# First batch of a banded attention with a feed-forward layer: attention weights and x turned on TensorE in float32, float32 weighted sums

## The chip, the cores and the metric

The kernel runs on one core of a Trainium2 chip. The metric is the device time of one execution in microseconds. Engines are named as the profile names them: PE (TensorE matmuls), PEld (its weight loads), DVE (VectorE), ACT (ScalarE), POOL (GpSimd), SP (the queue that issues the DMAs).

## The reference

Four batches of 768 tokens, 8 heads of 64 columns, then a feed-forward layer with 2048 hidden columns on all 3072 tokens. Cut to what matters:

```python
scores = scale * q @ k.T + bias            # bias: -slope[h] * distance
scores = where(is_global | is_local, scores, -1e9)   # 8 first keys, and the 96 before a row
a = exp(scores - max(scores))
a = a / (sum(a) + 1e-9)
x = a @ v                                  # (3072 tokens, 512 columns)
h = x @ w_in                               # 512 x 2048
g = h * tanh(log1p(exp(h)))
out = g @ w_out                            # 2048 x 512
```

The two weights of the feed-forward layer reach the kernel as 64-bit words and are turned into two float16 halves on the chip.

## The kernel before

**Tiles.** The tokens are worked in 12 chunks of 256 (`ci` 0 to 11), three to a batch. In a chunk there are two blocks of 128 rows and 8 heads, that is 8 attention tiles of 128 rows and two heads each: `t` runs from 0 to 95, and `t` 0 to 23 is the first batch. A row sees one or two windows of 128 keys (`nk`: the block's own 128, and a gathered window of the 96 before and 32 first ones; only the first block of a batch has one alone). The feed-forward layer has 8 units to a chunk, `m` = 8 ci + fp, 96 in all; it needs 32 pieces of weights, 0.5 MB each: an even piece belongs to w_in, an odd one to w_out.

**One order, written by hand.** A string, `PROGRAM`, holds some 2,100 tokens, a letter and a number each; every token issues one step, and each engine executes its instructions in the order in which the tokens stand. A dash behind a token puts a step on DVE that else stands on ACT (copies) or POOL (subtractions). The letters that are spoken of below:

- `q` loads q and k, `v` loads v, `w` a piece of the weights; all DMAs are issued by SP.
- `h`, `l`: v as two float16 halves (ACT L150, DVE L216). `x`: the gathered window of v, copied by DMA from those halves and from the window before.
- `s`: scores of two tiles on PE (L377); in the first batch (`ci < CF32`, 3) one float32 product of q and k, in the others three float16 products of halves.
- `t`: bias and row maximum (DVE L391). `y`: exponential and row sum (ACT L400), which leaves the attention weights `A` in float32.
- `g`, `p`: `A` as two float16 halves `hl` (a copy on ACT L150 or DVE L148; a subtraction on POOL or DVE, both L154).
- `X`: `hl` turned by one transposing DMA into `AT` (L420). `W`: the weighted sum on PE, three float16 products for each head and window (L436), into the PSUM tile `pav`.
- `R`: division by the row sum, which leaves x in float32 (DVE L443, L445, L447). `T`, `U`: its two float16 halves `xhl`. `V`: `xhl` turned by a transposing DMA into `xT` (L464).
- `A`, `S`, `B`, `C`: a piece of the weights joined from its words into float32 (L150, L319 or L317, L323, L327). `D`, `E`: its two halves (L150 or L148; L154).
- `i`: the first layer of a unit on PE, 24 products into a PSUM tile `ph` (L481). `j u n r G H`: the activation (ACT L488 to L500, DVE L504, L508). `z`, `Z`: its halves. `o`: the second layer, 12 products (L526), into `po0`, `po1`, or for `ci` 1 into the `pav` tiles.

**PSUM.** `sc` and `ph` have two tiles each in rotation, `pav0`, `pav1`, `po0`, `po1` one each.

**The start.** All weights must be made from words once, and the first batch's attention lies beside that. On PE the first-batch steps stand ahead of most of the feed-forward units: when the unit step `o8` begins, PE has issued all of `s` 0 to 22, `W` 0 to 23, and the units' steps `i0 o0 i8 i1 i9`. The same set, plus the new steps, stands ahead of `o8` in the changed order too.

Of the kernel before, what the change touches and what calls it, by code (L numbers as in the profile page):

```python
# [114 lines left out]
def windowed(st, tc, loc):  # L115
# [447 lines left out]
    def checks(i):  # L563
# [39 lines left out]
        p15' t16 E2 p14 t17 E5' X13 X15 X14 i0 W13 s18 W14 W10 W15 q5 y16 y17 g16' R2 p16 E3 w7 w9 X16 j0 u0 n0 r0 g17 T2 p17 t18 t19 B6 G0 H0 U2 x2 s20 y18
        z0 A6 S6 y19 A7 A9 g18 g19 R3 B7 t21 S7' T3' B9 C6 U3 p18' t20 p19' D4 y21 S9 D6 y20 Z0 E4 X17 V2 X18 V3 o0 s22 W17 W16 W18 i8 w8 g21' C9 p21 t23 C7
        t22 D9 g20 D7 y22 y23 E6 p20' N0 X19 X21 X20 w10 B8 E7' g23' p23 A8 S8 j8 g22 u8 n8 r8 G8 p22 E9 i1 W21 W20 W19 i9 X23 X22 w11 w12 R4 H8 j1 T4 C8 U4
        G1 D8' z8 u1 S10 n1 A10 j9 u9 r1 n9 r9 S11 A11 A12 S12 W23 W22 Z8 E8 R5 B10 C10 w14 w13 w24 w25 w16 w15 D10' H1 G9 z1' B11 H9 C11 o8 E10 i2 i10 j2
# [207 lines left out]
```

## Time and profile before

| | |
|---|---|
| median of 3 runs | 643.12 us (643.02 to 644.0) |
| the profiled execution, its own time | 643.97 us |
| its span in the trace | 642.2 us |
| PE, DVE, ACT, POOL busy | 596.2, 466.7, 455.7, 171.9 us |
| matmul records | 5042, of which L481 2304, L526 1152, L436 1056 |
| DMA, all queues | 80.38 MB in 152,680 packets, 121,376 of them under 512 B |

The profiled execution stands 0.85 us above the median. Of an engine's share of busy time little can be read alone here, since the first 160 us of the span and the rest have different limits; the table of stretches that the prediction shows is the view to begin with.

### The profile page before, as it was taken

The page shows a single profiled execution, that of the slowest core. Times are in us where ns is not written, and L with a number is a line of the kernel's source. Part 1 is how long each engine was busy: PE and PEld are TensorE (multiplying, and loading weights), DVE is VectorE, ACT ScalarE, POOL GpSimd, SP SyncE. Part 2 cuts the span into 40 slices and gives each one's busy share as a digit, 9 for nine tenths or more (in the row PEclk, how much of TensorE's full clock was granted, in tenths as well). Part 3 has the DMA queues.
Part 4 walks back from the last instruction along what each step waited for, and adds up shares of the span by engine and source line. Part 5 has one row for each costly group of instructions (what it writes and reads, how often), then busy time and mean ns, then how long its engine had stood idle before and what let it go on. Part 6 is the DMA issues. An engine that isn't in the chain of part 4 may idle for free.

```text
span 642.2 us, 13678 instructions
## 1 busy us (share of the span) xinstructions
PE 596.2 (93%) x5042; PEld 403.3 (63%) x5042; DVE 466.7 (73%) x1207; ACT 455.7 (71%) x1109; POOL 171.9 (27%) x144
## 2 busy tenths in 40 slices
PE   3746888999999999999999999999999999999996
PEld 2535565656666677576766766666767666667672
DVE  6798899999968678885567879368786685552443
ACT  4658897977977768687687785667768778554651
POOL 1233363423122321340332221121213244111020
PEclk9999899999999999999999999999999999999998
DMA  8999999247526569445458539244424456510001
GB/s 224 255 216 217 222 306 347 57 143 195 141 66 136 120 126 207 90 96 137 79 108 181 138 76 209 66 85 109 67 50 100 66 83 117 87 12 1 34 2 36
DMA packets 152680, 80.38 MB, mean 125 GB/s; under 512 B 121376, under 2 KB 141856, under 8 KB 152608
## 3 DMA queue, kind: packets, MB, share of 16 engines
q1 hardware_dynamic: 152608, 79.46, 54.6%
q8 instruction: 40, 0.66, 0.4%
q14 instruction: 32, 0.26, 0.1%
HBM read 38.54 MB, written 6.29 MB: 70 GB/s over the span
## 4 chain that ended last, share of the span: by engine, by line
PE 69%; DVE 12%; DMA 6%; ACT 5%; issue 4%; SPq 2%; POOL 1%; DVEq 0%; POOLq 0%; ACTq 0%
PE po L526 30%; PE ph L481 30%; PE sc L377 5%; DMA AT<-hl 4%; PE pav L436 4%; DMA kr<-kd 2%; DVE gf L508 2%; DVE ws L327 1%; DVE ws L323 1%; DVE A L391 1%; SPq L420 1%; ACT A L400 1%; ACT e L488 1%; ACT u L492 1%; PE pav L526 1%
## 5 line engine op out<-in xcount | busy, mean ns | idle before, releaser
L481 PE MATMUL ph<-xT,wts 128*128 128x256 f16 x2304 | 265.1, 273 | 2.1 <-POOL wts L154 1.3
L481 PEld LDWEIGHTS <-wts 128*128 128x128 f16 x2304 | 222.6, 98 | 39.5 <-POOL wts L154 2.6
L526 PE MATMUL po<-wts,gt 128*128 128x512 f16 x1056 | 241.7, 381 | 0.9 <-POOL gt L154 0.7
L526 PEld LDWEIGHTS <-gt 128*128 128x128 f16 x1152 | 109.6, 98 | 130.5 <-POOL gt L154 5.5
L154 POOL TENSOR_TENSOR gt<-gf,gt 128x512 f16<-128x512 f32 x58 | 72.2, 1246 | 212.4 <-DVE gt L148 95.5
L488 ACT ACTIVATE e<-ph 128x512 f32<-128x512 f32 x96 | 56.6, 590 | 89.6 <-PE ph L481 88.8
L508 DVE CUSTOM_DVE_ANT_0 gf<-gf,r 128x512 f32<-128x512 f32 x96 | 78.2, 816 | 50.2 <-ACT r L500 46.5
L154 POOL TENSOR_TENSOR hl<-A,hl 128x512 f16<-128x512 f32 (+1 forms) x51 | 59.2, 1163 | 191.0 <-DVE hl L148 98.3
L400 ACT ACTIVATE A<-A,nm 128x256 f32<-128x256 f32 (+1 forms) x192 | 91.5, 478 | 23.3 <-DVE nm L391 22.8
L504 DVE SCALAR_TENSOR_TENSOR gf<-e,ph 128x512 f32<-128x512 f32 x96 | 65.1, 681 | 32.4 <-ACT e L488 32.3
L391 DVE CUSTOM_DVE_ANT_0 A<-sc,mb 128x256 f32<-128x256 f32 (+1 forms) x192 | 68.4, 395 | 27.0 <-PE sc L377 24.8
L500 ACT ACTIVATE r<-r 128x512 f32<-128x512 f32 x96 | 60.0, 625 | 2.1
L492 ACT ACTIVATE u<-e 128x512 f32<-128x512 f32 x96 | 60.1, 626 | 1.9
L496 ACT ACTIVATE r<-u 128x512 f32<-128x512 f32 x96 | 59.8, 624 | 2.0
L436 PEld LDWEIGHTS <-AT 128*128 128x128 f16 x1056 | 40.3, 101 | 31.6 <-DMA AT<-hl 21.2
L436 PE MATMUL pav<-vc,AT 128*128 128x64 f16 x480 | 34.5, 198 | 13.1 <-DMA AT<-hl 12.5
L436 PE MATMUL pav<-vo,AT 128*128 128x64 f16 x576 | 40.2, 199 | 4.0 <-DMA AT<-hl 3.3
L150 ACT ACTIVATE gt<-gf 128x512 f16<-128x512 f32 x44 | 27.3, 622 | 19.6 <-DVE gmax L508 18.4
L377 PE MATMUL sc<-kr,qr 64*128 64x256 f32 (+1 forms) x96 | 24.5, 571 | 16.5 <-DVE nm L391 8.2
L154 DVE TENSOR_TENSOR hl<-A,hl 128x512 f16<-128x512 f32 (+1 forms) x45 | 34.3, 763 | 6.4 <-ACT hl L150 6.1
L154 POOL TENSOR_TENSOR wts<-ws,wts 128x512 f16<-128x512 f32 x20 | 26.5, 1332 | 46.4 <-DVE wts L148 23.4
L400 ACT ACTIVATION_READ_ACCUMULATOR A<-A,nm 128x1 f32 x192 | 36.0, 187 | 0.0
(96 smaller groups left out, 522.3 us busy)
## 6 DMA issues: line engine op xcount, KB each, us to landing
kr<-kd SPq DMA_DIRECT2D x32, 208.0 KB, 4.1
qr<-qT SPq DMA_DIRECT2D x24, 256.0 KB, 3.3
wts<-w_in SPq DMA_DIRECT2D x12, 512.0 KB, 5.9
vr<-v SPq DMA_DIRECT2D x12, 512.0 KB, 4.6
wts<-w_out SPq DMA_DIRECT2D x12, 512.0 KB, 7.6
out<-ob SPq DMA_DIRECT2D x11, 512.0 KB, 3.6
vc<-vo SPq DMA_DIRECT2D x20, 192.0 KB, 3.0
kr<-kd SPq DMA_DIRECT2D x16, 144.0 KB, 3.9
```

The lines of the kernel that those rows point to most:

```text
L154: (nc.vector if other else nc.gpsimd).tensor_tensor(out, in_, high, op=ALU.subtract)
L391: nc.vector.tensor_tensor_reduce(out=A[:, j, 0:w], in0=sc[j][:, 0:w], in1=m, scale=-1.0 / (UNIT if ci < CF32 else UNIT * SQ), scalar=3.0e3 ...
L400: nc.scalar.activation(A[:, j], A[:, j], AF.Exp, bias=nm[:, h:h + 1], scale=-1.0, accum_out=rs[:, h:h + 1])
L436: nc.tensor.matmul(pav[:, cols], AT[:, (x * 2 + j) * nk + kk, :], vs[kk][:, y, cols], start=(n == 0), stop=(n == last))
L481: nc.tensor.matmul(ph[:, j, :].rearrange("p (b t) -> p b t", b=2), wv4[:, 2 * fb, x, c * P:(c + 1) * P], xT[:, :, y * NCC + c, :], start=( ...
L488: nc.scalar.activation(mish[m]["e"], mish[m]["h"], AF.Exp, scale=-1.0 / (SV * SW), accum_out=esum[:, m:m + 1])
L492: nc.scalar.activation(u, mish[m]["e"], AF.Square, bias=0.5)
L496: nc.scalar.activation(mish[m]["r"], mish[m]["u"], AF.Ln, bias=0.25 / RS, scale=1.0 / RS)
L500: nc.scalar.activation(r, r, AF.Exp, scale=-1.0)
L504: nc.vector.scalar_tensor_tensor(gf, mish[m]["e"], 0.5, mish[m]["h"], op0=ALU.add, op1=ALU.mult)
L508: nc.vector.tensor_tensor_reduce(out=gf, in0=gf, in1=mish[m]["r"], scale=SG / (SV * SW * RS), scalar=0.0, op0=ALU.mult, op1=ALU.max, accum ...
L526: nc.tensor.matmul(pos[ci][t], gt[:, x, j, t * P:(t + 1) * P], wv4[:, 2 * fb + 1, y, :], start=(fb == 0 and n == 0), stop=(fb == NFB - 1 a ...
```

## The change

For the chunks of the first batch (`ci < CF32`) alone:

- `g`, `p` and `X` are gone. A new step `P` turns `A` in float32 on PE (`turn_p`): a product with an identity matrix for each head and window, 128 x 128, two for a tile with one window and four for the others, 88 in all. The result goes to PSUM: `po0` and `po1` in turn for `t` below 16, a `ph` tile for `t` 16 to 23. A new step `F` copies it from there to `AT` in SBUF, on ACT, or on DVE with a dash.
- `W` makes one float32 product for each head and window (88 in all) where three float16 ones stood (264).
- `h` and `l` are gone. `v` loads into the tile that `W` reads, and `x` loads the gathered window from HBM with two or three DMAs. The factor of 256 that `h` applied is now applied in `R`.
- `V` is gone. A new step `O` turns x in float32 on PE into a `ph` tile, four products for a block of rows, 24 in all; `T` and `U` make the halves from that tile and write `xT`.
- A new step `I` makes the identity matrix on DVE.

In the built program each of the turns is one weight load and one matmul, and each float32 product, of `s` as of `W`, is two loads and two matmuls. The later batches keep their steps. The order of the tokens is another one: far from the old one up to the second batch, then with a few neighbours swapped; on PE it is the same from `W40` on.

PE, the program's first instructions. Before (`sc` are scores; AT is the turned weights):

```order
L377 MATMUL sc<-kr,qr 128x128 x4
L377 MATMUL sc<-kr,qr 128x256 x4
L436 LDWEIGHTS AT
L436 MATMUL pav_214<-vo,AT 128x64
```

and of the change:

```order
L399 MATMUL sc<-kr,qr 128x128 x4
L452 MATMUL po_177<-idn,A 128x128 x2
L399 MATMUL sc<-kr,qr 128x256 x4
L452 MATMUL po_186<-idn,A 128x128 x2
L474 MATMUL pav_210<-vo,AT 128x64 x2
L452 MATMUL po_213<-idn,A 128x128 x4
L399 MATMUL sc<-kr,qr 128x128 x4
L452 MATMUL po_224<-idn,A 128x128 x4
L474 MATMUL pav_245<-vc,AT 128x64
```

What PE did alone, scores and sums, is now in three steps: a turn stands between a tile's scores and its sum, and the next tile's scores stand between its turn and its sum.

SP, from the first loads on. Before:

```order
L172 DMA qr<-qT 128x2x256
L175 DMA kr<-kd 64x2x288 x2
L292 DMA wts<-w_in 128x4x256
L206 DMA vr<-v 128x2x512
L294 DMA wts<-w_out 128x1024
L420 DMA_TRANSPOSE AT<-hl 128x4x128
L420 DMA_TRANSPOSE AT<-hl 128x8x128
L226 DMA vc<-vo 96x1024
L227 DMA vc<-vo 32x1024
```

(rows that repeat are left out) and of the change:

```order
L172 DMA qr<-qT 128x2x256
L175 DMA kr<-kd 64x2x288 x2
L314 DMA wts<-w_in 128x4x256
L209 DMA vo<-v 128x2x512
L229 DMA vc<-v 96x512
L230 DMA vc<-v 32x512
L316 DMA wts<-w_out 128x1024
L232 DMA vc<-v 96x2x512
L234 DMA vc<-v 32x512 x2
```

The transposing DMAs, each of which stood in SP's queue until its `hl` was made, are gone from the first batch; what stands there now reads HBM and waits for no engine but for a free buffer.

DVE, around the second pair of tiles. Before (`hl` are the halves of A):

```order
L391 ISA A,nm_182<-sc,mb 128x256
L391 ISA nm_182 128x1
L216 SCALAR_TENSOR_TENSOR vo<-vr,vo 128x2x512
L148 TENSOR_SCALAR hl<-A 128x512
L154 TENSOR_TENSOR hl<-A,hl 128x512
L317 TENSOR_SCALAR ws<-wts 128x512
```

and of the change:

```order
L413 ISA A,nm_196<-sc,mb 128x256
L413 ISA nm_196 128x1
L148 TENSOR_SCALAR AT<-po_186 128x256
L148 TENSOR_SCALAR AT<-po_213 128x512
L345 TENSOR_SCALAR ws<-wts 128x512
```

The copy into halves, the subtraction and the work on v have become copies out of PSUM.

```diff
     def load_v(ci):
-        vr = raws.tile([P, 2, DM], F32, name="vr", bufs=1)
+        if ci < CF32:
+            vr = vown[ci] = stk.tile([P, 2, DM], F32, name="vo")
+        else:
+            vr = vraw[ci] = raws.tile([P, 2, DM], F32, name="vr", bufs=1)
...
     def window_v(ci):
+        vc = stk.tile([P, 2, DM], F32, name="vc")
+        if ci < CF32:
+            far = L.v[b, 0:NGMAX, :]
+            if c == 0:
+                nc.sync.dma_start(vc[0:NPREV, 1], L.v[b, P - NPREV:P, :])
+                nc.sync.dma_start(vc[NPREV:P, 1], far)
+            else:
+                nc.sync.dma_start(vc[0:NPREV], L.v[b, c * CH - NPREV:(c + 1) * CH - NPREV, :].rearrange("(t p) m -> p t m", p=P)[0:NPREV])
+                for t in range(2):
+                    nc.sync.dma_start(vc[NPREV:P, t], far)
+            vcmp[ci] = vc
+            return
...
+    def identity(i):
+        nc.vector.tensor_scalar(idn, rel[:, P:W], 0.0, None, op0=ALU.is_equal)
...
+    def turn_p(t):
+        nk = shape(t)[-1]
+        A, n = pend[t], t
+        turn = ps.tile([P, 2, CH], F32, name="ph") if t >= 2 * 8 else ps.tile([P, DM], F32, name=f"po{t % 2}", bufs=1).rearrange("p (j t) -> p j t", j=2)
+        turn = turn.rearrange("p j t -> p (j t)").rearrange("p (k t) -> p k t", t=P)
+        for j in range(2):
+            for kk in range(nk):
+                nc.tensor.transpose(turn[:, j * nk + kk, :], A[:, j, kk * P:(kk + 1) * P], idn)
+        pend[t] = turn[:, 0:2 * nk, :]
+
+    def turned(t, other=False):
+        nk = shape(t)[-1]
+        AT = at.tile([P, 8, P], F16, name="AT", bufs=4).rearrange("p a t -> p (a t)").bitcast(F32).rearrange("p (a t) -> p a t", t=P)
+        copy(AT[:, 0:2 * nk, :], pend[t], 1.0, other)
+        pend[t] = AT
...
     def weigh(t):
+            if ci < CF32:
+                for kk in range(nk):
+                    nc.tensor.matmul(pav[:, cols], AT[:, j * nk + kk, :], vs[kk][:, cols], start=(kk == 0), stop=(kk == nk - 1))
+                continue
...
     def rows(n):
-        nc.vector.tensor_tensor_reduce(out=x, in0=pav.rearrange("p (h d) -> p h d", d=D), in1=ri.unsqueeze(2).broadcast_to([P, H, D]), scale=1.0, scalar=0.0, op0=ALU.mult, op1=ALU.max, accum_out=xmax[:, n:n + 1])
+        nc.vector.tensor_tensor_reduce(out=x, in0=pav.rearrange("p (h d) -> p h d", d=D), in1=ri.unsqueeze(2).broadcast_to([P, H, D]), scale=SV if ci < CF32 else 1.0, scalar=0.0, op0=ALU.mult, op1=ALU.max, accum_out=xmax[:, n:n + 1])
...
+    def turn_x32(n):
+        xf, = xhls.pop(n)
+        turn = ps.tile([P, 2, CH], F32, name="ph").rearrange("p j t -> p (j t)").rearrange("p (k t) -> p k t", t=P)
+        for c in range(NCC):
+            nc.tensor.transpose(turn[:, c, :], xf[:, c * P:(c + 1) * P], idn)
+        xhls[n] = turn
...
     def high_x(n, other=False):
+        if ci < CF32:
+            copy(xTs[ci][:, blk, 0:NCC, :], xhls[n], 1.0, other)
+            return
...
     def low_x(n):
+        if ci < CF32:
+            nc.vector.tensor_tensor(xTs[ci][:, blk, NCC:, :], xhls.pop(n), xTs[ci][:, blk, 0:NCC, :], op=ALU.subtract)
+            return
...
     acts = {
+        "I": identity, "P": turn_p, "F": turned, "O": turn_x32,
...
     PROGRAM = """
-        q0 q2 w0 v0 w1 s0 K0 L1 K1 L0 t0 L2' M7' L3 y0 M6' t1 g0' A0 y1 p0 g1 M2' M3' X0 s2 q1 t3 M0' M1' t2 h0 y2 L5 S1 y3 M5 l0 g2' p2' L4' p1 X1 q3 W0 s4
+        q0 s0 w0 v0 x0 q1 q2 w1 I0 f0 K0 L0 L1' K1 L3 M3 M7 L5 M1' L2' t1 L4' M0' t0 y1 y0 P1 s2 P0 F1' M6' S0' M2' t3 t2 F0' y3 y2 L6 W1 P3 s4 P2 L7 F3' t5
...
```

More of the change, by code (lines that the diff above doesn't have):

```diff
@@ L218, in window_v @@
     def window_v(ci):
-        c = ci % NCHB
+        b, c = divmod(ci, NCHB)
+        vc = stk.tile([P, 2, DM], F32, name="vc")
[10 more added lines that the diff above has]
+            return
         vo = vown[ci]
-        vc = stk.tile([P, 2, 2, DM], F16, name="vc")
+        vc = halves_v(vc)
         for t in range(2):
@@ L240, in windowed @@
     k0 = mt.tile([P, P], F32, name="r")
+    idn = cp.tile([P, P], F32, name="idn")
+    def identity(i):
+        nc.vector.tensor_scalar(idn, rel[:, P:W], 0.0, None, op0=ALU.is_equal)
     def masks_own():
@@ L446, in rows @@
         x = at.tile([P, H, D], F32, name="x", bufs=1)
-        nc.vector.tensor_tensor_reduce(out=x, in0=pav.rearrange("p (h d) -> p h d", d=D), in1=ri.unsqueeze(2).broadcast_to([P, H, D]), scale=1.0, scalar=0.0, op0=ALU.mult, op1=ALU.max, accum_out=xmax[:, n:n + 1])
+        nc.vector.tensor_tensor_reduce(out=x, in0=pav.rearrange("p (h d) -> p h d", d=D), in1=ri.unsqueeze(2).broadcast_to([P, H, D]), scale=SV if ci < CF32 else 1.0, scalar=0.0, op0=ALU.mult, op1=ALU.max, accum_out=xmax[:, n:n + 1])
         xhls[n] = (x.rearrange("p h d -> p (h d)"),)
+    def turn_x32(n):
[3 more added lines that the diff above has]
+            nc.tensor.transpose(turn[:, c, :], xf[:, c * P:(c + 1) * P], idn)
+        ci, blk = divmod(n, 2)
+        if ci not in xTs:
+            xTs[ci] = at.tile([P, 2, 2 * NCC, P], F16, name="xT", bufs=3)
+        xhls[n] = turn
     def high_x(n, other=False):
+        ci, blk = divmod(n, 2)
+        if ci < CF32:
+            copy(xTs[ci][:, blk, 0:NCC, :], xhls[n], 1.0, other)
+            return
         xf, = xhls[n]
@@ L603, in windowed @@
[L603 to L606, printed above, removed]
@@ new lines, in windowed @@
+        j62 t72 u62 U17 z61 t73 V17 n62 Z61' r62 s74 G62 j63 v11 o60 a23' y72 c21' y73 t74 g72' g73 H62 u63 p72 o61 z62 X72 n63 Z62' y74 t75 x10 y75 g74'
+        p73' p74 s76 i64 r63 t76 t77 X73 y77 G63 y76 H63 X74 W72 d21' g76 o62 j64 p76 u64 g75' X76 z63 p75 n64 g77' r64 i65 X75 b23 G64 H64 Z63' W73 s78
+        p77' X77 o63 t78 a24 j65 z64' b24 u65 t79 n65 G65 y78 i66 r65 H65 z65' g78' W76 j66 W75 p78 s80 Q7 W74 t81 Z64 i67 X78 u66 c22' y79 t80 g79 n66 p79'
+        s82 r66 Z65' X79 W77 j67 o64 y80 y81 g80' G66 g81' o65 H66 R18 z66 u67 Z66 p81' n67 i68 r67 T18' p80' U18 X80 W78 X81 W79 R19 o66 G67 T19 j68 H67
```

109 lines of the change are left out of this document (55 added, 54 removed).

## The prediction

> **What bounds the kernel now.** The page comes first: its busy times, and the span in 40 slices of 16 us.
>
> ```profile
> PE 596.2 (93%) x5042; PEld 403.3 (63%) x5042; DVE 466.7 (73%) x1207; ACT 455.7 (71%) x1109; POOL 171.9 (27%) x144
> PE   3746888999999999999999999999999999999996
> DVE  6798899999968678885567879368786685552443
> DMA  8999999247526569445458539244424456510001
> ```
>
> PE is full from the eighth slice to the last but one, so most of the span is PE's own work. Only the start is another stage: PE has holes, DVE is near its limit from the third slice to the eleventh, and the DMA engines are full for six. The change works in that stage alone, so the table by stretches is read next (columns: stretch, length, then PE, PEld, DVE, ACT, POOL busy with their counts, the clock, DMA share, GB/s).
>
> ```profile
> 0.00:20.00 20.00, 7.02 (x32) 5.20 (x34) 13.67 (x57) 9.42 (x29) 3.31 (x10) 1.00 0.89 223
> 20.00:40.00 20.00, 14.14 (x110) 10.45 (x109) 15.42 (x53) 13.35 (x40) 6.32 (x6) 1.00 1.01 233
> 40.00:60.00 20.00, 11.13 (x100) 8.41 (x97) 17.02 (x44) 15.69 (x44) 5.13 (x5) 1.00 1.00 218
> 60.00:80.00 20.00, 15.75 (x152) 10.15 (x148) 17.62 (x52) 16.23 (x43) 8.07 (x7) 0.91 1.09 233
> 5.10:86.60 81.50, 53.12 (x468) 38.33 (x469) 67.78 (x208) 59.32 (x163) 26.90 (x23) 0.98 1.04 233
> 86.60:159.20 72.60, 68.34 (x475) 43.18 (x471) 71.10 (x138) 61.12 (x120) 28.23 (x21) 1.00 0.69 213
> 159.20:642.00 482.80, 474.79 (x4110) 321.74 (x4106) 326.01 (x859) 334.00 (x827) 115.94 (x93) 1.00 0.45 94
> ```
>
> I cut at 86.6 us because there the unit step `o8` begins, and ahead of it PE has the same steps in both orders (and `P` and `O` in the new one):
>
> ```profile
> 86.62 2.75 PE L526 MATMUL pav<-wts,gt 128*128 128x512 f16 x12
> ```
>
> Behind 159.2 us PE is idle for 8.0 us of 482.8: nothing to win. From 86.6 to 159.2 it is idle for 4.1 us, and DVE for 1.5 (71.10 of 72.60): both are at their limit. Ahead of 86.6 PE works 53.1 us of 81.5 and DVE 67.8, so DVE is nearer to its limit there. What ends PE's holes, and two of the other engines', is read from the waits of the first 170 us (us in total, times, the longest):
>
> ```profile
> PE pav L436 <- DMA AT<-hl: 14.9, 10, 5.2
> PE sc L377 <- DVE nm L391: 8.2, 7, 2.0
> PE sc L377 <- DMA kr<-kd: 6.7, 4, 5.2
> ACT wc L150 <- DMA wts<-w_in: 4.0, 3, 2.4
> DVE A L391 <- PE sc L377: 3.6, 4, 1.0
> ```
>
> The longest wait is for the turned attention weights, the very transfer that goes. But it is not worth 14.9 us: where the transfer is gone, PE next stands before DVE's work. So the forecast goes by DVE first, and is then tested on PE.
>
> **DVE, ACT and POOL.** The rows are those of the first 87 us (the POOL and L436 rows those of the first 160, where no later step has joined them):
>
> ```profile
> L148 DVE TENSOR_SCALAR hl<-A 128x512 f16<-128x512 f32 (+1 forms) x10 | 4.0, 408 | 4.0 <-DMA AT<-hl 3.9
> L154 DVE TENSOR_TENSOR hl<-A,hl 128x512 f16<-128x512 f32 (+1 forms) x9 | 7.3, 812 | 2.2 <-ACT hl L150 2.1
> L216 DVE SCALAR_TENSOR_TENSOR vo<-vr,vo 128x1024 f16<-128x1024 f32 x3 | 3.8, 1267 | 1.1 <-ACT vo L150 1.1
> L504 DVE SCALAR_TENSOR_TENSOR gf<-e,ph 128x512 f32<-128x512 f32 x3 | 2.0, 672 | 0.0
> L150 ACT ACTIVATE hl<-A 128x512 f16<-128x512 f32 (+1 forms) x14 | 8.0, 579 | 6.5 <-issue 5.8 <-DMA AT<-hl 0.4
> L150 ACT ACTIVATE vo<-vr 128x1024 f16<-128x1024 f32 x3 | 3.1, 1036 | 0.0
> L488 ACT ACTIVATE e<-ph 128x512 f32<-128x512 f32 x4 | 2.4, 588 | 0.6 <-PE ph L481 0.6
> L154 POOL TENSOR_TENSOR hl<-A,hl 128x512 f16<-128x512 f32 (+1 forms) x15 | 16.5, 1106 | 39.5 <-DVE hl L148 16.2 <-ACT hl L150 16.2 <-DVE mb L148 3.6
> L323 DVE TENSOR_SCALAR ws<-wts 128x512 uint16<-128x512 uint16 x10 | 5.2, 526 | 0.5 <-DMA wts<-w_in 0.5
> L327 DVE SCALAR_TENSOR_TENSOR ws<-wc,ws 128x512 int32<-128x512 int32 x10 | 7.9, 801 | 0.0
> ```
>
> DVE loses 4.0 (ten copies `g`), 7.3 (nine `p`) and 3.8 (`l`): 15.1 us. It gains nine copies `F` out of PSUM. No row has one: its bounds are a copy between SBUF tiles, 0.41 us, and L504, which reads a PSUM tile of that size, 0.67; I take 0.67, since what F reads is PSUM: 6.0 us, and 0.3 for the identity (L323's 0.53 is above it). Net -8.8 us. ACT loses 8.0 and 3.1 and gains fifteen `F` at L488's 0.59: 8.9; net -2.2. POOL loses 16.5. `T` and `U` stay in number and size.
>
> The order spends some of this. Ahead of `o8` it now has fifteen `B` for twelve, fourteen `C` for twelve, and other weight steps that went from ACT and POOL to DVE, while two `H` and one `G` stand later: with L323, L327 and L504 that is 3 x 0.53 + 2 x 0.80 + about 2 for the rest - 3 x 0.67, an estimate of +3.2 us. So DVE has 8.8 - 3.2 = 5.6 us less ahead of `o8`. If its idle time stays (13.7 us from 5.1 to 86.6), `o8` begins at 81.0.
>
> **PE.** Here the time of a float32 step must be found, and the trace has two prices for it:
>
> ```profile
> 5.15 0.50 PEld L377 LDWEIGHTS sc<-kr,qr 64*128 64x128 f32 x2 [5.15 <-DMA qr<-qT]
> 63.09 0.29 PEld L377 LDWEIGHTS sc<-kr,qr 64*128 64x128 f32 x2 [1.63 <-DVE ws L323]
> 51.90 2.08 PE L377 MATMUL sc<-kr,qr 64*128 64x256 f32 x8
> 59.21 1.14 PE L377 MATMUL sc<-kr,qr 64*128 64x256 f32 x8
> L377 PEld LDWEIGHTS sc<-kr,qr 64*128 64x128 f32 x72 | 13.8, 319 | 15.6 <-DVE nm L391 8.6 <-DMA qr<-qT 5.1 <-DMA kr<-kd 1.0
> L377 PEld LDWEIGHTS sc<-kr,qr 64*128 64x128 f32 x8 | 0.7, 186 | 0.1
> 22.89 0.67 PEld L436 LDWEIGHTS <-AT 128*128 128x128 f16 x12 [0.73 <-DMA AT<-hl]
> 58.75 0.41 PEld L436 LDWEIGHTS <-AT 128*128 128x128 f16 x12 [1.89 <-DMA AT<-hl]
> L436 PE MATMUL pav<-vo,AT 128*128 128x64 f16 x144 | 12.2, 217 | 4.0 <-DMA AT<-hl 3.3 <-DVE vo L216 0.8
> L436 PE MATMUL pav<-vc,AT 128*128 128x64 f16 x120 | 10.1, 213 | 12.2 <-DMA AT<-hl 11.6 <-DMA vc<-vo 0.6
> ```
>
> The same eight scores take 2.08 us at 51.9 and 1.14 us at 59.2, and a load 319 ns before 54 us and 186 from 55 to 62. The clock column says 1.00 for both, yet by durations PE runs at about half rate until `i0` begins and at full rate from then on. [...]
>
> A float32 load follows the one before it after 0.50 - 0.32 = 0.18 us at half rate and 0.29 - 0.19 = 0.10 at full. A float32 product of `W` is two loads, and its 64 columns stream in less: 0.36 or 0.20 us. Below, it could go at the pace of float16 loads (0.67 and 0.41 us for twelve: 0.056 and 0.034 apiece, twice); above, like a product of 256 columns (2.08 / 4 = 0.52; 0.29). A turn is one load and one matmul: 0.18 or 0.10, with bounds of 0.056 and 0.034 below and half a scores product, 0.26 and 0.15, above. [...]
>
> Ahead of `o8` stand 88 products and 108 turns. If PE stays at half rate until `i0` (32 products, 48 turns) and is at full rate from there (56, 60): 11.5 + 11.2 + 8.6 + 6.0 = 37.3 us for 22.3 of L436. PE's 53.1 us become 68.1. At half rate throughout: 31.7 + 19.4 = 51.1, and PE has 81.9; at full rate 28.4, and 59.2.
>
> With 68.1 us PE has 13.4 us of holes left in 81.5. Its holes now, without those for AT, are 28.4 - 14.9 = 13.5. If all of these stayed, `o8` would not move. But the waits for `sc` tiles (8.2) arise where PE has nothing but the next scores to go to; turns and longer sums now fill part of them. I let half of them go: 4.1 us, and `o8` comes at 5.1 + 68.1 + 13.5 - 4.1 = 82.6. DVE's figure is 81.0; the later one counts, so -4.0.
>
> **SP and DMA.** The 24 transposes at L420 and six at L464 leave a DMA system that is full (1.04). The new loads of v and windows are smaller than what goes and stand early. I count this at nothing: weights that land sooner are work for a DVE that is full. If that cover were gone, the most to be won is ACT's 4.0 us of waiting for weights; and if the loads of v came late instead, the first sums would wait for them as they did for k, up to 5.2 us. The factor in `R` rides on an instruction that is there anyway.
>
> **Behind o8.** `O5` adds 4 x 0.10 = 0.4 us. PE's 4.1 us of holes there are waits for halves of weights and of g; DVE being two pieces of weights ahead, I take 1.3 off. Sum: -4.0 + 0.4 - 1.3 = -4.9 us. The span becomes 637.3, and that execution's own time 643.97 - 4.9 = 639.1; it stood 0.85 above the median of 643.12, so the forecast is 638.2.
>
> **Rivals.**
>
> Slower: PE becomes the bound of the start, at half rate. The new chain (scores, exponential, turn, copy, sum) is a round trip from PE and back for each tile, with two `po` or `ph` tiles to hold it, and from `t` 16 on the turns share `ph` with the units and the x turns, so a hole of PE can wait for `G` or `F` of the tile before. If holes keep the rate at half until `o8`, PE has 81.9 us of work by the sum above, the units at half rate not counted; with 5.1 at the start and half of the 13.5 us of holes it begins `o8` at 93.8, +7.2, and after the same gains behind it the time is about 649.4. It decides from about 76 us of work on (81.5 less those 6.8, plus 1.3 won later). Against it: float32 work keeps PE busier than the 14.1 us of 20 it has now from 20 to 40. [...]
>
> No change: both views give the same `o8`, as the sum with 13.5 us of holes does. 643.1.
>
> Much faster: PE wakes early. With the full rate from about 20 us, PE's 59.2 us leave DVE alone as the bound, DVE's own waits (13.7 us idle, of which 3.9 for AT buffers and 3.6 for scores at L391) shrink by half, and POOL, 16.5 us lighter, no longer holds the halves of weights back: 5.6 + 6.9 + 2 - 0.4, about 14 us, 629.
>
> **How the numbers follow.** Forecast 638.2 with a chance of 0.42, its own range 634 to 641; much faster 0.19; no change 0.13; slower 0.26. To leave out no more than 2 in 10 the range goes from 629 to 651. Faster by over 0.2% (about what a measurement of this kernel can tell from no change, 1.3 us) takes the forecast and the first rival: 0.60; within it 0.13; slower 0.27.
>
> **What would show it.** `o8` near 82 us; DVE ahead of it about 62 us busy; the wait of `pav` for AT gone from DMA and come back, smaller, behind ACT or DVE; loads of about 0.3 us early and 0.19 later; a turn at 0.10 to 0.18 us. Wrong would be the steps on PE if a product of `W` takes over 0.4 us at full rate, or if waits of turns for a `ph` or `po` tile exceed 8 us; the step on DVE if it is as busy as before ahead of `o8`.

## The result, and the profile after

The changed kernel takes 626.13 us (median of four runs, 624.53 to 629.82) where the kernel before took 643.56 beside it (643.02 to 644.49): ratio 0.974, interval 0.969 to 0.978. It is 17.4 us faster. The forecast was 4.9 us faster, with 629 us as the fast end of its range: the direction was right, the size was not.

The profiled execution has an own time of 625.97 us and a span of 624.2. The page's busy times and slices of 15.6 us:

```profile
PE 605.9 (97%) x5066; PEld 418.3 (67%) x5066; DVE 448.8 (72%) x1192; ACT 451.3 (72%) x1109; POOL 154.2 (25%) x130
PE   5999999989999999999999999999999999999996
DVE  6999998995798677884659796657785685542443
DMA  8997763422595574748088668045342256300001
```

PE is half empty in the first slice and full from there (an 8 in the ninth, where `o6` waits); before, it had holes in the first seven. The stretches (columns as before: length, then PE, PEld, DVE, ACT and POOL busy with counts, the clock, DMA share, GB/s), the first of them up to the moment at which `o8` begins:

```profile
0.00:20.00 20.00, 12.29 (x74) 9.18 (x74) 13.95 (x66) 10.32 (x39) 0.85 (x7) 1.00 0.90 248
20.00:40.00 20.00, 19.61 (x168) 17.32 (x168) 18.87 (x65) 19.53 (x54) 3.48 (x3) 1.00 1.08 289
40.00:60.00 20.00, 19.80 (x153) 15.52 (x152) 18.85 (x64) 19.81 (x57) 4.86 (x4) 1.00 0.88 275
5.10:70.60 65.50, 62.31 (x488) 52.07 (x489) 60.16 (x209) 58.73 (x168) 12.26 (x10) 1.00 0.90 260
70.60:143.30 72.70, 69.36 (x475) 44.92 (x474) 69.34 (x141) 60.83 (x126) 26.71 (x21) 0.98 0.45 136
143.30:624.00 480.70, 474.20 (x4107) 321.34 (x4105) 317.61 (x835) 330.45 (x815) 114.41 (x92) 1.00 0.46 95
```

```profile
70.62 0.59 PE L586 MATMUL pav<-wts,gt 128*128 128x512 f16 x2
```

`o8` begins at 70.6 us instead of 86.6: 16.0 of the span's 18.0 us are won ahead of it. Behind it the span lasts 553.6 us; before it was 555.6. Ahead of it PE works 62.3 us of 65.5, so it is idle for 3.2 us where it was idle for 28.4. PE's waits in the first 170 us (total, times, the longest):

```profile
PE sc L399 <- DMA kr<-kd: 5.9, 2, 5.2
PE po L452 <- ACT A L422: 1.8, 1, 1.8
PE po L586 <- DVE wts L154: 1.3, 1, 1.3
PE po L586 <- DVE wts L148: 1.2, 1, 1.2
```

The 14.9 us for AT and the 8.2 us for `nm` are gone, and nothing has come in their place: the first row is the load of the first keys, the second the first exponential, and the last two stand at `o6`, 135 us into the span.

### The profile page after: what moved, and what is told of

Same layout as the page of the kernel before. It is cut to its first block, busy times and chain, and to the rows that moved or that the text cites. A ratio compares the mean times of both kernels' runs of the same rounds, so it can differ in the third digit from the quotient of the medians.

```text
span 624.2 us, 13611 instructions
## 1 busy us (share of the span) xinstructions
PE 605.9 (97%) x5066; PEld 418.3 (67%) x5066; DVE 448.8 (72%) x1192; ACT 451.3 (72%) x1109; POOL 154.2 (25%) x130
## 4 chain that ended last, share of the span: by engine, by line
PE 79%; DVE 11%; DMA 5%; ACT 3%; issue 2%; DVEq 0%; ACTq 0%
PE po L586 34%; PE ph L541 34%; PE sc L399 5%; PE pav L478 4%; DMA wts<-w_out 3%; DVE ws L349 2%; DMA qr<-qT 2%; DVE ws L345 1%; DVE wts L154 1%; DVE gf L564 1%; PE pav L586 1%; DVE A L413 1%; PE po L452 1%; DVE gf L568 1%; DVE ws L339 1%
## 5 line engine op out<-in xcount | busy, mean ns | idle before, releaser
L413 DVE CUSTOM_DVE_ANT_0 A<-sc,mb 128x256 f32<-128x256 f32 (+1 forms) x192 | 68.0, 396 | 24.5 <-PE sc L399 22.7
L154 POOL TENSOR_TENSOR hl<-A,hl 128x512 f16<-128x512 f32 (+1 forms) x37 | 44.1, 1197 | 147.7 <-DVE hl L148 93.6
L154 POOL TENSOR_TENSOR wts<-ws,wts 128x512 f16<-128x512 f32 x17 | 21.3, 1260 | 75.8 <-ACT wts L150 56.1
L150 ACT ACTIVATE gt<-gf 128x512 f16<-128x512 f32 x41 | 25.3, 620 | 13.5 <-DVE gmax L568 12.3
L478 PEld LDWEIGHTS <-AT 128*128 128x128 f16 x792 | 28.7, 98 | 6.9 <-issue 2.1
L154 DVE TENSOR_TENSOR gt<-gf,gt 128x512 f16<-128x512 f32 x37 | 27.3, 739 | 3.8 <-ACT gt L150 3.6
L489 DVE CUSTOM_DVE_ANT_1 x<-pav,ri 128x512 f32<-128x512 f32 x24 | 16.6, 691 | 17.4 <-PE pav L478 15.0
L148 DVE TENSOR_SCALAR hl<-A 128x512 f16<-128x512 f32 (+1 forms) x37 | 15.6, 424 | 17.8 <-ACT A L422 13.2
L399 PE MATMUL sc<-wc,ws 64*128 64x256 f16 (+1 forms) x432 | 28.1, 262 | 0.1
```

The lines of the kernel that those rows point to most:

```text
L154: (nc.vector if other else nc.gpsimd).tensor_tensor(out, in_, high, op=ALU.subtract)
L399: nc.tensor.matmul(sc[j][:, a2, 0:w], x[half, a2, rows_], y[half, a2, col0:col0 + w], start=(n == 0), stop=(n == len(terms) - 1))
L413: nc.vector.tensor_tensor_reduce(out=A[:, j, 0:w], in0=sc[j][:, 0:w], in1=m, scale=-1.0 / (UNIT if ci < CF32 else UNIT * SQ), scalar=3.0e3 ...
```

## The experiments

Each run is compared with runs of the kernel before that were timed beside it (their medians lie between 643.6 and 645.7 us). The table holds what was measured. `o8` and the first record of full rate are read from the trace of the profiled execution, which is one of the runs and can stand off the median: its own time is 634.2 us in e7, 650.4 in e10, 666.9 in e9, 627.2 in e12 and 623.7 in e14. In e2, e3, e8 and e12 the first full rate lasted for 3.4 us only; in e12 it came back for good at 15.2 us, in e3 from 21.1 to 48.5.

| run | median, us | ratio to before, interval | `o8` begins | full rate first recorded |
|---|---|---|---|---|
| before | 643.56 | | 86.6 | 54.9 |
| after | 626.13 | 0.974 (0.969 to 0.978) | 70.6 | 14.6 |
| e1 new steps, old order | 683.46 | 1.056 (1.052 to 1.061) | 119.2 | 39.0 |
| e2 old steps, new order | 689.35 | 1.067 (1.064 to 1.070) | 132.3 | 25.0 |
| e3 before, PE filled | 645.2 | 0.999 (0.998 to 1.001) | 87.9 | 10.9 |
| e4 after, PE warmed | 627.24 | 0.973 (0.967 to 0.979) | 69.8 | 10.7 |
| e5 = e1, PE filled | 679.34 | 1.053 (1.050 to 1.057) | 112.1 | 27.5 |
| e6 after, PE filled | 635.94 | 0.986 (0.984 to 0.989) | 79.8 | 13.2 |
| e7 after, one hole | 630.19 | 0.978 (0.975 to 0.980) | 77.9 | 22.4 |
| e8 = e2, old loads | 695.38 | 1.077 (1.074 to 1.081) | 137.0 | 27.9 |
| e9 = e1, late copies | 671.28 | 1.043 (1.040 to 1.045) | 102.3 | 27.6 |
| e10 after, x by DMA | 645.96 | 1.001 (1.000 to 1.003) | 89.0 | 21.9 |
| e11 after, windows from SBUF | 631.42 | 0.979 (0.977 to 0.981) | 74.8 | 22.7 |
| e12 after, mended and warmed | 625.04 | 0.970 (0.967 to 0.972) | 72.0 | 4.9 |
| e13 after again | 630.21 | 0.978 (0.976 to 0.980) | 73.9 | 22.1 |
| e14 after, mended | 625.88 | 0.972 (0.969 to 0.974) | 70.5 | 13.9 |

### Steps and order apart: e1 and e2

My prediction took the steps as the gain and the order as a cost. e1 keeps the steps and undoes the order, e2 the reverse. The start of `PROGRAM` in the kernel before, in e1, in the changed kernel and in e2:

```
before  y0 M6' t1 g0' A0 y1 p0 g1 M2' M3' X0 s2 q1 t3
e1      y0 M6' t1 P0  A0 y1 F0' P1 M2' M3'   s2 q1 t3
after   t0 y1 y0 P1 s2 P0  F1'   M6' S0' M2' t3 t2 F0'
e2      t0 y1 y0 g1 s2 g0' p1 X1 M6' S0' M2' t3 t2 h0 p0 X0
```

> The new steps (turns on TensorE, float32 sums, v from HBM) in the order of the kernel before: each turn P stands where the copy g stood, each copy F where the rest p stood, O ahead of T; a few steps stand later where a tile must come free first. It splits the change into its steps and its order. Theory 'the steps': the gain of 17 us comes from work and waits that are gone, so most of it stays without the new order: 626 to 632 us, o8 begins at 71 to 77 us, full clock from about 15 us. Theory 'the order': the new steps alone give what my sum gave for DVE and PE in the order they had, about 5 us: 636 to 640, o8 at 81 or later. If turns that stand right behind their exponential hold PE up, it can also come out near 643.

> The steps of the kernel before (halves g and p, DMA transposes, float16 sums, v split) in the order of the changed kernel: g where the turn P stood, p and the DMA transpose where the copy F stood, h, l and x ahead of the first sum of their chunk. Theory 'the steps': the order without the steps has no use, since the sums still wait for AT by DMA (14.9 us before): 641 us or slower, o8 at 85 us or later. Theory 'the order': well below 643, some 632 to 638.

No theory had this size: each half of the change alone costs some 40 us (e1 37.8, e2 43.7), and both together win 17. For e2 the first theory's "641 us or slower" came true, but nothing in it led to 689. In e2 the sums wait for AT by DMA, for 50.4 us:

```profile
PE pav L436 <- DMA AT<-hl: 50.4, 11, 19.9
```

SP's queue in e2 shows why (start, length, the issue):

```profile
17.17 4.77 SPq L420 DMA_TRANSPOSE AT<-hl  x2
22.00 0.58 SPq L292 DMA_DIRECT2D wts<-w_in  x1
...
34.96 2.03 SPq L175 DMA_DIRECT2D kr<-kd  x2
37.53 3.40 SPq L420 DMA_TRANSPOSE AT<-hl  x2
```

No transpose is issued between 22 and 37.5 us, since the new order puts the loads of weights, q and k in a row. The two transposes that stand behind these loads are issued from 37.5 us on, behind the last of them (34.96 to 36.99).

In e1, from 40 to 120 us, DVE is busy for 8 to 14 us of each 20, PE for 14 to 18, and the clock is at half for 44 of these 80 us. Three of the four stretches:

```profile
40.00:60.00 20.00, 16.35 (x81) 14.17 (x81) 14.39 (x48) 11.29 (x33) 1.23 (x1) 0.65 0.54 163
80.00:100.00 20.00, 16.23 (x92) 10.27 (x88) 9.50 (x27) 9.93 (x28) 4.62 (x4) 0.74 0.00 1
100.00:120.00 20.00, 14.19 (x102) 11.97 (x102) 8.28 (x20) 10.09 (x25) 1.16 (x1) 0.74 0.15 53
```

What DVE and ACT wait for there, in the first 120 us:

```profile
DVE AT L148 <- PE ph L452: 12.8, 3, 7.9
DVE AT L148 <- PE po L452: 6.0, 3, 4.2
ACT xT L150 <- PE ph L496: 14.4, 3, 6.8
ACT AT L150 <- PE po L452: 13.9, 6, 4.8
```

They wait for turns, 47.1 us in these four rows. Where `p` stood in DVE's or ACT's queue, and needed only what those engines had made, `F` now stands, and needs a turn that PE has queued behind other work. Two causes are thus possible for e1: the clock, or these waits. In PE's time both show:

```profile
5.10:119.10 114.00, 89.28 (x488) 69.83 (x489) 56.43 (x195) 53.96 (x157) 8.43 (x8) 0.81 0.50 143
```

The steps ahead of `o8` that take PE 62.3 us in the changed kernel take 89.3 here, and its holes are 24.7 us instead of 3.2. Of the 48.5 us by which `o8` is late, 27.0 are slower work and 21.5 are holes.

### The clock against the waits: e3, e5, e9

e3 fills PE in the kernel before, e5 does it in e1, e9 moves only the copies of e1:

```diff
 e3:  -W0                 +<4 idle matmuls> W0      (also ahead of s2 ... s16)
 e5, in turn_p and turn_x32, ahead of the turns:
+     for _ in range(2):
+         nc.tensor.matmul(turn, warm[:, 0:P], warm, start=True, stop=True)
 e9:  -o0 s22 W17 W16 W18 i8 w8 P21 C9 F21' t23 C7 t22
      +o0 s22 W17 W16 W18 F19 i8 w8 P21 C9 t23 C7 t22 ... P20 F21' P23
```

> The kernel before, with four float16 matmuls of 512 columns that compute nothing ahead of each weighted sum and each pair of scores before i0 (20 x 4, 17 us at full rate, in a stretch where PE has some 22 us of holes). It tells what a busier PE alone is worth, without any of the change. Theory 'the clock': full rate from about 15 us on; the eight products of 256 columns take 1.1 us then, and o8 comes 3 to 6 us earlier: 637 to 641 us. Theory 'DVE and the transfers bound the start': PE's rate is worth nothing there: 642 to 646, o8 at 86 to 89.

e3 takes the same time as the kernel before, although its PE has full rate from 21.1 to 48.5 us. PE's wait for AT shrinks to 10.8 us and `o8` stands where it stood, a little later. So a faster PE alone won nothing there. The added matmuls are work on PE too (65.9 us ahead of `o8` instead of 53.1), so what the rate gave and what they cost cannot be told apart.

> The new steps in the old order (683.5 us, with the clock at half in most of its first 119 us) with two float16 matmuls of 512 columns that compute nothing ahead of each turn P and each O, in the tile that the turn then writes: 30 x 2, 13 us at full rate, 26 at half. They only add work to PE's queue; what they can give is the clock. Theory 'the rate': full rate early and kept, and the time falls far in spite of the added work: 640 to 660 us, o8 at 80 to 95. Theory 'the chain' (turns that stand right behind their exponential hold PE up, the rate follows from that and decides nothing): the fillers are added to the path: 690 to 710.

The rate comes at 27.5 us and stays until 75.3, `i0` begins at 57.5 us instead of 66.4, and yet the whole is only 4 us faster, between the two ranges.

```profile
5.10:112.10 107.00, 87.52 (x546) 63.60 (x547) 55.98 (x195) 53.88 (x157) 8.49 (x8) 0.94 0.53 152
```

By the starts of PE's instructions the added matmuls take some 17 us of these 87.5, so the steps themselves fell from 89.3 to some 71. With full rate from 27.5 to 75.3 us the steps take some 18 us less, and the added matmuls cost nearly as much. The holes stay, 19.5 us, and the faster clock did not remove them. One piece of e5 in PE's queue, and then the DVE row that waits for it:

```profile
78.14 4.71 PE L594 MATMUL po<-wts,gt 128*128 128x512 f16 x12
...
86.57 2.78 PE L549 MATMUL ph<-xT,wts 128*128 128x256 f16 x24
...
89.62 0.60 PE L457 MATMUL ph<-idn,A 128*128 128x128 f32 x4
```

```profile
90.26 0.69 DVE L150 TENSOR_SCALAR AT<-ph 128x512 f32<-128x512 f32 x1 [8.93 <-PE ph L457]
```

DVE stands still for 8.9 us in front of `F21`, whose turn is queued on PE behind `o0`, `s22`, three sums and `i8`; the maxima and weight pieces behind `F21` stand too, and at 97 us PE waits for DVE's part of the activation (`gf`) for 5.3 us.

> The new steps in the old order once more (683.5 us), without fillers, with one edit: each of the 24 copies F stands as late in the order as its tile and its sum allow, instead of where the rest p stood. In the run with fillers DVE stood still for 8.9 us at one F (its turn P21 stood on PE behind o0, s22, three sums and i8), with t, C and G queued behind that F. Theory 'copies that wait for PE hold DVE and ACT up': DVE's waits for turns shrink and the time falls well below 683: 655 to 672 us. Theory 'the turns hold PE up' (P right behind its exponential): the copies make no difference, 678 to 688.

671.3 us, 12 us faster than e1, just inside the first theory's range:

```profile
5.10:102.30 97.20, 75.01 (x488) 60.78 (x489) 55.90 (x195) 53.84 (x157) 8.47 (x8) 0.91 0.59 168
```

DVE's waits for turns that are to be copied fall from 18.8 us to 2.0. PE's holes hardly shrink, from 24.7 us to 22.2, but its work falls from 89.3 to 75.0, with full rate from 27.6 us. So copies that wait are a real part of e1's loss, and in these two profiles they cost mainly by way of PE's rate: waits and clock are not two separate causes. `o8` is still 31.7 us later than in the changed kernel, 12.7 by PE's work and 19.0 by its holes. How the holes divide among turns that hold PE up and loads that come late (the DMA share is near nothing from 80 to 120 us in e1) no run here separates.

### The loads in e2: e8

```diff
-W0 W2 g4 w2 v1 q3 w4 w7 w3 w5 q4 w6 w10 q5 B0 M4' t6
+W0 W2 g4 v1 B0 M4' t6 A0 y6 S1 p5 t7 y7 X5 p4' X4 w2 w3 s8
```

> The old steps in the new order again (689.4 us), but the loads of weights, q and k stand among the DMA transposes in SP's queue as they did in the kernel before. In the run with the new order's loads no transpose was issued from 22 to 37.5 us, while SP issued 14 such loads in a row. Theory 'the loads in the queue': most of the loss comes from there: 645 to 660 us. Theory 'order as a whole' (sums stand too near their transposes for the latency of these): still over 670.

Later loads move in the same way, and with them the steps that make those weights. It is 695.4, no better. The wait for AT falls to 38.8 us and its longest to 6.2, so the burst of loads did cause the 20 us stalls, but other waits grow as much:

```profile
PE pav L436 <- DMA AT<-hl: 38.8, 11, 6.2
PE sc L377 <- DVE nm L391: 17.1, 5, 10.8
```

My theory of the loads falls as the explanation of the 44 us. That the order as a whole sets its sums too near to the turns for a transposing DMA fits the 11 waits that are left, but no run shows it by itself.

### Is PE the bound of the new start? e4, e6, e7

```diff
 e4:  -s0                  +<11 idle matmuls> s0 <4 idle matmuls>
 e6:  as e5, in the changed kernel
 e7:  -s10                 +<matmul; 4 memsets of its operand on POOL; matmul> s10
```

> The changed kernel with the same two matmuls ahead of each turn P and each O: 30 x 2 of 0.22 us, 13 us more on PE, of which some 11 between 10 and 70 us where PE has 3 us of holes. Theory 'PE bounds the start of the changed kernel': nearly all of it is paid: o8 at 79 to 83, 635 to 639 us. Theory 'DVE and ACT bound it, PE's queue only waits along' (DVE has 5.3 us idle ahead of o8, ACT 6.8): PE takes it into time that DVE needs anyway: 626 to 631, o8 at 71 to 75.

635.9 us, as the first theory said, and `o8` 9.2 us later. PE is busy for 73.0 of 74.7 us:

```profile
5.10:79.80 74.70, 73.02 (x546) 57.42 (x547) 62.51 (x210) 60.55 (x169) 12.35 (x10) 1.00 0.84 230
```

So PE bounds the start of the changed kernel, and DVE, at 62.5 us busy, is only the second.

> The changed kernel, with eleven matmuls that compute nothing ahead of the first scores and four behind them, in PE's empty first 5.2 us and its wait of 1.8 us behind s0. They make PE busy earlier and add nothing to the path. Theory 'PE bounds the start of the changed kernel, and its rate decides': full rate from about 5 us instead of 14.6, up to 3.8 us of PE work saved (7.6 us at half rate become 3.8): 622 to 624 us, o8 at 67 to 69. Theory 'DVE, ACT and the loads bound its first 15 us': no change, 625 to 627, o8 at 70 to 71.

No change in time. The added matmuls push `s0` back by 1.0 us (to 6.1), and full rate comes at 10.7 instead of 14.6; at `o8` 0.85 us is left of that. PE's waits in the first 10 us are those for the keys and the first exponential, so its rate there is worth little.

> The changed kernel with one hole in PE's work ahead of s10 (22.9 us): a matmul, four memsets on the idle POOL that wait for it (0.53 us each), and a matmul that waits for them: 2 to 3 us in which PE stands still, once. Theory 'one hole costs the clock': half rate follows for two to six windows of 3.4 us, 3 to 10 us more PE work on top of the hole: 631 to 639 us, o8 at 76 to 83. Theory 'the rate holds or comes back at once': the hole and no more: 627 to 630, o8 at 72 to 74.

630.2 us lies between the two ranges, and by itself it tells nothing, for e13 below has the same. The trace, of the execution that took 634.2 us, tells more. The hole, and the scores behind it:

```profile
29.05 0.23 PE L595 MATMUL ph<-warm 128*128 128x128 f16 x1 [2.65 <-POOL warm L594]
29.21 2.08 PE L401 MATMUL sc<-kr,qr 64*128 64x256 f32 x8
```

After a hole of 2.65 us the eight products take 2.08 us, which is half rate (1.13 at full rate, in e13); the records show half rate for 3.4 us, 29.2 to 32.6, and full rate from there. Against the changed kernel `s8` is already 3.4 us late, since full rate came only at 22.4 us; `s12` is 8.0 us late: 3.4, 2.9 for the hole with its matmuls, and 1.6 for the 3.4 us at half rate. `o8` is 7.3 us late. So this one hole costs itself and 1.6 us by the half rate behind it.

### When full rate comes: e13

> The changed kernel again, unchanged, as the neighbour of the next run and for a second look at when its full rate begins. In three runs whose queue on PE was the same as the changed kernel's up to 14.8 us, PE's full rate began at 22 us and not at 14.6. Theory 'the moment differs from execution to execution': the times spread over some 5 us as they did (624.5 to 629.8), and the profile may show 14 to 23 us, with o8 between 70.6 and 74.7. Theory 'it belongs to the kernel': full rate from 14.6 us again, o8 at 70.6.

The same program again: 630.2 us. Its five times lie between 629.3 and 631.7, a smaller spread than the first theory expected, but all above the first median of 626.1. Its profile has full rate from 22.1 us. The same step `s6`, and then `s8`, in this execution, and after them its stretch up to `o8`:

```profile
18.64 2.08 PE L399 MATMUL sc<-kr,qr 64*128 64x256 f32 x8
...
23.18 1.13 PE L399 MATMUL sc<-kr,qr 64*128 64x256 f32 x8
```

```profile
5.10:73.90 68.80, 65.59 (x489) 54.76 (x490) 60.11 (x209) 58.93 (x168) 12.27 (x10) 1.00 0.85 248
```

In the first execution `s6` took half of that:

```profile
16.83 1.13 PE L399 MATMUL sc<-kr,qr 64*128 64x256 f32 x8
```

PE's queue ran alike in both up to 14.8 us, without a hole from 9.7 on. In one, full rate began at 14.6, in the other at 22.1: 7.5 us longer at half rate, 3.3 us more PE work (65.6 for 62.3), and `o8` 3.3 us later (73.9), while DVE's work is the same. So the moment is not a property of the kernel alone, and 3.3 us of the gain hang on it. Of six profiles in which PE's queue is the same up to 14.8 us (after, e7, e10, e11, e13, e14), two had 14 us and four had 22.

The traces record the moments at which the clock changes: 14.63, 137.51 and 140.92 us in the first profile, 54.86, 65.10 and 68.52 in the kernel before. The steps between them are 122.88 and 3.41 us in the one, 10.24 and 3.41 in the other, all whole multiples of 3.413. They do not say what differs at the start: from the last hole (until 9.7 us) PE works without a hole in both executions, and full rate comes after 4.9 us in the first and after 12.4 in e13. What sets the moment, no run shows.

### Two parts undone: e10 and e11

```diff
 e10: -R1 C2 T0 y11 y10 s12 O1 W8 ... T1 D2 U0 U1 A4 ... E2 i0
      +C2 T0 y11 y10 s12 W8 ... D2 U0 R1 T1 V0 U1 V1 A4 ... E2 i0   (O0 to O5 gone)
 e11: -nc.sync.dma_start(vc[NPREV:P, 1], far)             # and the other loads of v from HBM
      +the copies from vo and the window before, as they are for later chunks
```

> The changed kernel with x of the first three chunks turned by the DMA transposes of the kernel before: no O, and V right behind U. PE has 24 turns less (2.4 us), SP six transposes more, and the first unit step i0 waits for a transpose (3.1 us from issue to landing at the least, more behind weight loads) where it waited for O and U. Theory 'a PE that is full pays for each wait': i0, i8 and what follows wait for xT, o8 at 72 to 78, 628 to 634 us. Theory 'x turned by PE is not part of the gain': 624 to 626.5, o8 at 68 to 70.5.

646.0 us: the whole gain is gone. I had put 8 us at most on it. One wait takes most of it:

```profile
46.85 5.30 PE L533 MATMUL ph<-xT,wts 128*128 128x256 f16 x24 [12.49 <-DMA xT<-xhl]
```

```profile
34.44 2.85 SPq L175 DMA_DIRECT2D kr<-kd  x2
37.50 7.33 SPq L516 DMA_TRANSPOSE xT<-xhl  x2
```

The first unit step begins at 31.5 us in the changed kernel. Here PE waits in front of it for 12.5 us: the halves of x are ready at 33.4 and 35.9, the two transposes are issued from 37.5 on, behind loads in SP's queue, and their issue alone takes 7.3 us. `i0` itself then takes 5.3 us instead of 3.1, in a stretch at half rate from 35.6 to 52.6 us. `o8` comes at 89.0 us, 18.4 later than in the first profile and 15.1 later than in e13, where full rate also began at 22 us. So in this order the early place of `i0` hangs on `O`. The edit also sets `R1` and `T1` later, and an order with the transposes ahead of those loads was not run, so 20 us is the price of this placement, not of every one.

> The changed kernel with the windows of v of the first three chunks copied from the tiles of v in SBUF (as in the kernel before, in float32), instead of loaded from HBM. SP's queue then stands at x until v has landed, and the window lands some 3 us after that. Theory 'the loads are hidden': 625 to 627.5, o8 at 70 to 72. Theory 'SP's queue and the first sums pay': W3 (15.9 us) or the weight loads behind x1 come late, and PE, which is full from 9.7 us, pays it whole: 628 to 636.

631.4 us, ratio 0.979; the changed kernel in e13 has 0.978. No difference that the times show, and `o8` is 0.9 us later than in e13: the windows' loads are hidden either way, or nearly. By its range alone it would have spoken for the second theory; its profile has full rate from 22.7 us, as e13's has from 22.1.

### A faster version: e12 and e14

In the changed kernel `o6` waits twice for one weight piece, and 3.4 us at half rate follow (137.5 to 140.9):

```profile
135.60 0.38 PE L586 MATMUL po<-wts,gt 128*128 128x512 f16 x1 [1.20 <-DVE wts L148]
137.28 3.39 PE L586 MATMUL po<-wts,gt 128*128 128x512 f16 x8 [1.30 <-DVE wts L154]
```

```diff
-g25 t26 t27 S27' B27 r14 A31 c8 j7 Z6 H14 C27 B29 D27' E27' z14
+g25 S27' B27 C27 D27' E27 t26 t27 r14 A31 c8 j7 Z6 H14 B29 z14
 e12 also: nine idle matmuls ahead of s0, four behind it
```

> A try at a faster version: the changed kernel, with the halves of one weight piece (C27, D27, E27, which o6 waits for at 133.6 to 137.3 us, with a window of half rate behind it) ahead of two pairs of maxima in DVE's queue, E27 on POOL, which is idle there; and nine matmuls that compute nothing ahead of s0 with four behind it. Theory 'a full PE gains what its waits lose': o6 loses its 2.5 us of waiting and 1.7 us of half rate less what the delayed G7 and H14 cost then, and the start gains 0 to 1: 621 to 624 us. Theory 'DVE is the bound there and the stall only moves': 625 to 627.

> The changed kernel with the one edit of order of the try before (C27, D27 and E27 ahead of two pairs of maxima, E27 on POOL), without the matmuls at the start. Theory 'a full PE gains what its waits lose': o8 to i17 and i16 shorter by 2.5 to 3.5 us, the time 2 to 3 us below the changed kernel of the same call. Theory 'the stall moves': within 1 us of it.

e14 in the trace:

```profile
134.88 2.33 PE L586 MATMUL po<-wts,gt 128*128 128x512 f16 x10 [0.83 <-POOL gt L154]
```

One wait of 0.83 us is left at `o6` (and one of 0.66 us is new ahead of `i16`), no half rate follows, and from `o8` to `i16` 72.6 us pass instead of 75.3 (both in the changed kernel and in e13): the 2.7 us that the first theory named. The times are 625.9 us beside 630.2 for the changed kernel timed next to it, ratios 0.972 (0.969 to 0.974) and 0.978 (0.976 to 0.980). So e14 is faster there; of its 4.3 us, 2.7 are the stall. The rest may be the moment of full rate, which puts `o8` 3.4 us apart in the two profiles; no run separates it. Against the first four times of the changed kernel (626.1 us, 0.974) the times alone show no gain, so the 2.7 us rest on the traces. e12, with the matmuls at the start added, has 0.970 (0.967 to 0.972): no further gain that its interval shows, and 625.0 us is outside the 621 to 624 that I expected.

## Why the prediction was right in direction and wrong in size

**Behind `o8`: right in size, not in reason.** I took -0.9 us behind `o8`; the profiles give -2.0 (first) and -0.9 (e13: 628.6 - 73.9 = 554.7). The 1.3 us that I took off there came from waits for weights, and these did not shrink as I said: `o6` still waits for 2.5 us.

**The prices on PE: right, but all a little low.** The rows of a sum (two products each) and of two tiles' turns at full rate:

```profile
18.71 0.39 PE L474 MATMUL pav<-vc,AT 128*128 128x64 f32 x2
18.93 0.39 PE L474 MATMUL pav<-vo,AT 128*128 128x64 f32 x2
...
20.99 1.09 PE L452 MATMUL po<-idn,A 128*128 128x128 f32 x8
21.92 0.33 PE L474 MATMUL pav<-vo,AT 128*128 128x64 f32 x2
```

A row of x2 is one float32 product, which leaves two records: 18.93 - 18.71 = 0.22 us, where I took 0.20. Eight turns take 21.92 - 20.99 = 0.93 us, 0.12 each with the change of step; I took 0.10. At half rate the two products of `W1` take 0.75 us from 12.97 to 13.72, 0.37 each (taken: 0.36), and a turn in e13 0.23, from 16.00 to 16.91 (taken: 0.18, upper bound 0.26). At 0.02 us for each of 88 products and 108 turns, that is an estimate of 4 us too little at full rate.

**The prices on DVE and ACT: right.** The copies `F` out of PSUM:

```profile
L150 ACT ACTIVATE AT<-po 128x512 f32<-128x512 f32 x8 | 4.6, 582 | 0.0
L148 DVE TENSOR_SCALAR AT<-po 128x512 f32<-128x512 f32 x4 | 2.8, 689 | 0.5 <-PE po L452 0.5
```

I had 0.59 and 0.67. DVE is busy for 60.2 us ahead of `o8`; I had 62.

**The first step that failed: PE's work of 68.1 us.** It holds two errors of opposite sign. One is the subtraction in "37.3 us for 22.3 of L436". The 22.3 is the sum of two rows, 12.2 and 10.1, whose records overlap in time. Taken together, L436 keeps PE busy for 13.6 us ahead of `o8`, and the scores (L377) for 24.5 (PE and PEld busy of the one line):

```profile
5.10:86.60 81.50, 13.57 (x264) 11.25 (x264) 0.98 1.04 233
5.10:86.60 81.50, 24.48 (x96) 16.48 (x96) 0.98 1.04 233
```

With 13.6 the sum is 53.1 - 13.6 + 37.3 = 76.8 us, and with my 9.4 us of holes `o8` would have come at 91.3, later than before. By its own prices the sum pointed to the rival "slower", which I had deciding from about 76 us on; that it gave a gain is luck.

The other error is "PE at half rate until `i0`". I took it from the kernel before, where full rate began with the first unit step, at 54.9 us. In the changed kernel it began at 14.6, and the work was 62.3 us, or 65.6 in e13. It reaches steps that I had left as they were. The same scores (now L399), of the first profile and of e13:

```profile
5.10:70.60 65.50, 15.20 (x96) 9.53 (x96) 1.00 0.90 260
5.10:73.88 68.78, 16.64 (x96) 10.44 (x96) 1.00 0.85 248
```

They fall from 24.5 us to 15.2; with the units' steps ahead of `o8` (11.4 and 4.3 us, now 11.1 and 2.8) work that did not change in number costs 11 us less. My sum gave the faster rate to new products and turns alone, and not before `i0`. From 76.8 to 62.3 is 14.5 us, of which the wrong subtraction hides 8.7: what is left to see is 5.8.

**The second: "half of the 8.2 us of waits for `sc` go, the rest of PE's holes stay".** I left 13.5 - 4.1 = 9.4 us of holes; 3.2 were measured, in both executions. That is 6.2 us. Work and holes together make up my whole error at `o8`: 82.6 - 70.6 = 12.0 = 5.8 + 6.2. The same assumption stood on DVE, "if its idle time stays (13.7 us)": it became 65.5 - 60.2 = 5.3. I treated holes as a property of the stage, when they belonged to an order made for transposing DMAs.

**Order as a cost.** I counted it as +3.2 us on DVE. e1 shows that the steps without it cost 38 us, and e2 that it is unusable without the steps, by 44. Both numbers are larger than anything in my sum, because my sum had only work and waits of the order before; a round trip from ACT to PE and back to DVE was in none of its terms. It stood in the rival "slower", and e1 is that rival come true: I had 81.9 us of work at half rate (90.6 with 13.6 for L436) and 6.8 of holes, and e1 has 89.3 and 24.7. DVE and ACT standing before turns are part of it, 12 us of the time by e9; the rest is not divided. In the changed kernel these waits are 1.2 us ahead of `o8`, where e1 has 47.1 in its first 120 us.

**SP and DMA at nothing.** For the windows of v this is right, or nearly (e11). For the x transposes it was wrong in kind: gone, they allow `i0` to stand at 31.5 us, and with them back, placed as in e10, PE waits for 12.5 us. A transfer that seemed hidden would not have been hidden in the order that its absence made possible.

**Which rival came.** "PE wakes early", 629 us with full rate from about 20 us and holes that shrink. e13's execution, with 22 us, took 630.4; that of the first profile, with 14.6, took 626.0. But that rival left DVE alone as the bound, and e6 shows that PE is; its 59.2 us of PE work had the wrong subtraction and the slow scores in it, so its number came near in part by luck. Given 0.19, it deserved more: the rows that I quoted for it (waits of PE and DVE for each other) were the same as those that I kept as holes.

**When full rate comes: not shown.** The rival "slower" let holes of PE keep the rate at half, and set against it that float32 work keeps PE busier. That holes and busy time decide the rate was my assumption. The first profile, with 4.9 us from the last hole to full rate, and e7, with 3.4 us at half rate behind its hole, fit it. e13, with 12.4 us at half rate and no hole, does not, and no run shows why.

## What to carry to other kernels

Where a change takes a transfer out of a chain, the order that was written around that transfer is part of the change: cost the new steps in the order that they allow, and look in each engine's queue for the steps that now wait for another engine. Here neither half was worth anything alone (38 and 44 us slower). Idle time of an engine that is about to become the bound is not a constant to be carried over; work out when it would be done without holes (here 62.3 to 65.6 us of work came, with 3.2 of holes where I had left 9.4) and give that case its own weight. Rows of one line that alternate overlap in time: take their common busy time from a table of stretches, not their sum (13.6 us here, not 22.3). And once PE is the bound, a hole can cost its length and a stretch at half rate behind it, as in e7 (2.65 us, and 3.4 us at half rate).

## What was not expected of the hardware

- The moment of full rate differs between two executions of one program by 7.5 us (14.6 and 22.1 us, with PE's work alike up to 14.8), and moves `o8` by 3.3 us. A comparison of this kernel within 1% needs the profile beside the times: e7 and e11 would have been misread without it.
- The clock column reads 1.00 until the first recorded change, also where durations show half rate (2.08 us for eight products of 256 columns in e13 at 18.6, 1.13 at 23.2).
- PE ran at half rate for over 11 us without a hole, twice: in e13 from 9.7 to 22.1 us, and in e1 from 27.7 to 39.0. In e1, a hole of 1.3 us ahead of `s12` (44.6), behind two of 0.4 and 0.9 us, was followed by half rate from 45.9 to 66.3.
- Half rate also came behind short holes: 1.2 and 1.3 us at `o6`, where the changed kernel then ran at half rate from 137.5 to 140.9. PE was busy for 0.91 us of the 3.41 ahead of that; for 1.51 us of the 3.41 ahead of the kernel before's half rate (65.1 to 68.5), and for 0.77 in e7 ahead of 29.2.
